# Handing the first stage's rows to the second stage inside SBUF, and one table tile behind the first weights

## The chip, the cores and the metric

The kernel runs on one core of one Trainium2 chip. The metric is the device time of one execution in microseconds. Five engines work side by side, each through its own instructions in order: TensorE (PE, matrix products), VectorE (DVE), ScalarE (ACT), GpSimd (POOL) and SyncE (SP). SP, ScalarE and GpSimd also issue transfers (DMA) between DRAM and SBUF, the memory on the core; products land in PSUM, a small memory of banks, and must be copied out ("evicted") from there.

## What is computed

```python
x = randn(8, 3008, 256) * 0.1          # batch, sequence, dimension
X = np.fft.fft(np.fft.fft(x, axis=1), axis=2).real        # FNet mixing
h = X.reshape(24064, 256) @ w_in                          # w_in 256 x 2048
g = h * np.clip(h + 3.0, 0.0, 6.0) / 6.0                  # hard swish
out = g @ w_out                                           # w_out 2048 x 256
```

So the kernel takes the real part of a two-dimensional Fourier transform of each of 8 sequences and sends all 24064 rows through a two-layer network. [...]

## The kernel before

**The stages.** The sequence length is 47 * 64. Stage 1 is a transform of length 47 over rows that are first folded (sums and differences of mirrored columns, on VectorE for the first sequence, on GpSimd later); its result z holds, in its partitions, the 48 rows (24 frequencies, real and imaginary) of two blocks, and for each of them some columns n2. Stage 2 is a transform of length 64 over n2, so it needs the n2 in the partitions: the rows change places. That is done by transfers: z goes to a DRAM tile zd and comes back as a tile g. Stage 2 multiplies g by a table T (one slice per group `gr` of frequencies; a slice for both sides of the frequency, with zeros in the quadrants that don't belong) and leaves q; the row qn is the last row of q, spread over all partitions. The transform along the 256 columns is folded into w_in (`fold_w_in`, by the table C), giving W1 and its last row WN, which `send_wn` sends from a row to a column by small transfers on SP.

**The network.** The rows are worked on in chunks (`Chunk`) of four frequencies, each in eight steps `fc` over the 2048 hidden columns. A step is `mlp1` (products u and v of W1 with q on TensorE, then `activate`: s, sum, difference and gates on VectorE, the relu on ScalarE, leaving a), `combine` (sums c of parts of a, on GpSimd) and `mlp2` (products of G, the turned w_out, with a and c). In the first chunk `mlp2_first` does without c.

**The weights.** The 16 pieces of w_in and w_out (`PIECES`: two of w_in, two of w_out, and so on) are loaded by `load_w(j)` and turned by five helpers, one for each engine's part: `exponent_a` (ScalarE, two passes of 128x512), `exponent_b` (two products on TensorE), `exponent_c` (a copy on ScalarE), `mantissa` (two passes on VectorE) and `join` (VectorE, gives wi or a block of G). `fold_w_in(j)` makes W1 of a piece of w_in.

**The order.** Nothing is scheduled automatically: `manual_schedule` keeps the order in which the program text issues instructions, engine by engine. The start-up is written out by hand: eight gathers of x (each 128 rows of 1024 floats) from GpSimd, folds on VectorE, four rounds of stage 1 (`FIRST`) with `evict_first` one round behind, then the exchange through DRAM, stage 2 of groups 0 and 1, and the first chunk's steps with the weight pieces between them (`first_steps`, `second_steps`). `beside(p)` lists what else is issued at which step: `put(t, f, ...)` at step t. `LATER` names the steps at which rows of later groups go from z to zd.

**What the change touches.** `evict_first` copies a round of stage 1 from PSUM to z (112 partitions) and sends the rows of groups 0 and 1 to zd at once, those of later groups when `LATER` says so. `load_g_half` reads a group of zd back into g. `both_tables` gives the slice of T for both sides. `load_t` loads a slice of T, for groups 0 and 1 from ScalarE's and GpSimd's queue in the start-up. `clear_table` writes the zero quadrants, for slices 0 and 1 on ScalarE. `keep_awake` are products of zeros that keep TensorE running. `spare` are two PSUM banks used by turns.

Of the kernel before, what the change touches and what calls it, by code (L numbers as in the profile page):

```python
# [7 lines left out]
F32 = mybir.dt.float32  # L8
# [50 lines left out]
def kernel(  # L59
# [30 lines left out]
    NG = NCK // 2  # L90
    NSG = 4
    NIX = NP * NXC
    DH = 32
# [162 lines left out]

    later, middle = {}, []

# [86 lines left out]
    def evict_first(hb, m, ps, pt):  # L345
        k = FIRST.index(m)
        pool, tag = ((zpool, "z"), (zpool, "z"), (apool, "a"), (cpool, "c"))[k]
        z = pool.tile([PX, 2, 2, D + 1], F32, tag=tag, name="z")
        for h in range(2):
            nc.scalar.copy(z[:, h, :, D:], pt[h][0:PX])  # L350
        nc.scalar.copy(z[:, 0, :, 0:D], ps[0][0:PX])
        (nc.vector.tensor_copy if k == NM - 1 else nc.scalar.copy)(z[:, 1, :, 0:D], ps[1][0:PX])
        if not first.zd:
            first.zd[0] = dpool.tile([NG, 2 * KK, 2, NS, D + 1], F32, tag="zd0", name="zd")
        zd = first.zd[0][:].rearrange("g k c (h n) d -> (g k c) h (n d)", h=2)
        n0 = 2 * 4 * KK
        for i in range(2):
            n = (m * XC + 2 * i) * (D + 1)
            for j in range(PZ // n0):
                dst = zd[j * n0:(j + 1) * n0, :, n:n + 2 * (D + 1)]  # L360
                rs = slice(i * PB + j, i * PB + 2 * n0, 2) if j < 2 else slice(i * PB + 2 * n0, i * PB + PZ)
                src = z[rs].rearrange("p h n d -> p h (n d)")
                if j == 0:
                    (nc.scalar if k == NM - 1 and i else nc.sync).dma_start(out=dst, in_=src)
                else:
                    later.setdefault((j, k), []).append((dst, src))

# [68 lines left out]

    def both_tables(gr, blk, u):
# [4 lines left out]
    def stage2_half(hb, gr, copy=nc.scalar.copy, ps=None):  # L442

        vg, i = hb.b * NSG // 2 + gr // 2, gr % 2
        if i == 0:
            first.q[vg] = qpool.tile([P, 2, 2 * TB], F32, tag="q", name="q")
        g = hb.g[gr]
        if starting[0] and ps is None:
            for u in range(KK):
                ps = bank([P, 2, P], "ps2")  # L450
                for blk in range(2):
                    nc.tensor.matmul(ps[:, blk].rearrange("p (b k) -> p b k", b=2),
                                     g[:, u, blk * (P + 1):blk * (P + 1) + P], both_tables(gr, blk, u),
                                     start=True, stop=True)
                copy(first.q[vg][:, :, u * P:(u + 1) * P], ps[:])
            return
        ps = bank([P, 2, TB], "ps2") if ps is None else ps
        for u in range(KK):
            for blk in range(2):
                nc.tensor.matmul(ps[:, blk, u * P:(u + 1) * P].rearrange("p (b k) -> p b k", b=2),  # L460
                                 g[:, u, blk * (P + 1):blk * (P + 1) + P], both_tables(gr, blk, u),
                                 start=True, stop=True)
        copy(first.q[vg][:, :, i * TB:(i + 1) * TB], ps)
# [13 lines left out]

    def spread_by_pe(hb, ps, copy=nc.scalar.copy):
        row_tile(first, 0)
        for u in range(KK):  # L480
            nc.tensor.matmul(ps[:, u * P:(u + 1) * P], hb.g[0][:, u, D:D + 1].to_broadcast([P, P]),
                             both_tables(0, 1, u), start=True, stop=True)
        copy(first.qn[0][:, 0:TB], ps)
        del hb.g[0]
# [273 lines left out]
    def exponent_b(j):  # L758
        pm = [PM[j % len(PM)][:, i].bitcast(F16) for i in range(2)]
        if j == 3:  # L760
            exs[j] = spare[1][:].rearrange("p i n -> p (i n)")
        elif starting[0] or j == 4:
            exs[j] = ps_h.tile([P, WB], F32, tag="uv", name="ex")[:]
        elif j % 2 == 0:
            exs[j] = bank([P, WB], "ex")[:]
        else:

            exs[j] = spare[1 if j % 4 == 1 else 0][:].rearrange("p i n -> p (i n)")
        for i in range(2):
            nc.tensor.matmul(exs[j], E[:, i], pm[i], start=(i == 0), stop=(i == 1))  # L770
# [42 lines left out]
    def fold_w_in(j):  # L813
# [7 lines left out]
        for blk in range(2):  # L821
            for i in range(2):
                nc.tensor.matmul(ps[:, blk], C[:, i, blk * P:(blk + 1) * P], wi[:, i], start=(i == 0), stop=(i == 1))  # L823
        (nc.vector.tensor_copy if j == 0 else nc.scalar.copy)(W1[:, :, fc * nb:(fc + 1) * nb], ps[:])
        for f in range(2 * fc, 2 * fc + 2):
# [85 lines left out]
    nc.gpsimd.dma_start(out=C[:], in_=c_dim)  # L911
# [12 lines left out]
    exponent_c(0)  # L924
    clear_table(1, slice(0, 2))
    for k, m in enumerate(FIRST):
# [5 lines left out]
    for k, m in enumerate(FIRST):  # L932
# [22 lines left out]
    join(1)  # L955
    see(w[PIECES[1]][:, 0:1])
    load_w(3)
    for j in range(4, 10):
# [12 lines left out]
    starting[0] = False  # L971
# [6 lines left out]
    def beside(p):  # L978
# [7 lines left out]
        if p == 0:  # L986
            for gr in range(2, NG):
                put(gr, load_t, gr)
            put(2, spread_half, halves[0], 1)
# [71 lines left out]

    def first_steps(s):
        j = 2 * s + 4
        more = j < len(PIECES)
        if s == 0:

            mlp2_first(*chunk(s), halves=(0,))
        else:
            mlp2_first(*chunk(s - 1), halves=(1,))
        if more:
            exponent_b(j)
            exponent_b(j + 1)
            exponent_c(j)
            if s > 0:
                join(j)
                tail(j + 1)  # L1080
                exponent_a(j + 2)
        if s > 0:
            mlp1(*chunk(s + 1))
        else:
            activate(*chunk(s + 1), *uv, between=lambda: join(j))
            tail(j + 1)
            exponent_a(j + 2)
        mlp2_first(*chunk(s), halves=(1,) if s == 0 else (0, 1))
        if s == 0:
            fold_w_in(j)  # L1090
        if more:
            exponent_b(j + 2)
            exponent_c(j + 2)
            exponent_a(j + 3)
            if s > 0:
                fold_w_in(j)
            fold_w_in(j + 1)
            if s > 0:
                exponent_b(j + 3)

# [30 lines left out]

    LATER = {1: ((1, 2), (2, 2)), 3: ((1, 0), (1, 1), (1, 3)), 5: ((2, 0), (2, 1), (2, 3))}

# [32 lines left out]
def _tables(B, S, D):  # L1166
# [18 lines left out]
    f0 = np.zeros((2, 64, 8, 64))  # L1185
    f0[:, :N1, :, :2 * NK1] = g[:, :, np.r_[np.arange(32).reshape(2, 16).T.ravel(), 32:2 * NK1]].swapaxes(0, 1)
    f[2:5:2] = f[2:5:2, ::-1]
# [5 lines left out]
    for i in range(B):  # L1193
# [22 lines left out]
    co, si = cs(np.outer(np.arange(D), np.arange(D)), D)  # L1216
    d = np.concatenate([co[:, :h], -si[:, 1:h], co[:, h:h + 1]], axis=1) / WS
    return {
        "c_stage1": f.astype(np.float32),
        "c_stage2": t.reshape(N2, 2, NK1 // 4, 4, N2).transpose(2, 0, 1, 3, 4).astype(np.float32),  # L1220
        "c_dim": d.reshape(2, h, D).swapaxes(0, 1).astype(np.float32),
    }
# [31 lines left out]
```

## Time and profile before

| | |
|---|---|
| median of 3 runs | 1931.37 us (1930.52 to 2507.39) |
| profiled execution, its own time | 1931.23 us |
| its span, first to last instruction | 1929.5 us |
| TensorE busy | 1914.8 us, 99% of the span |
| VectorE, GpSimd, ScalarE busy | 1429.4, 1448.3, 679.5 us |
| granted TensorE clock, mean | 0.999 |
| bytes moved | 98.22 MB, mean 51 GB/s |
| transfers in the first of 40 slices (48 us) | 270 GB/s |

The durations below come from the one profiled execution. A row of the timeline has the start in microseconds from the span's start, the time to the end of the group, the engine (with a q: its issuing of transfers), the line, the operation, what it writes and reads, and in brackets how long the engine had been idle and what ended that. Groups of small products overlap a little, so the start of the next group is the better measure of how long one takes. A row of waits has the total, the number and the longest.

### The profile page before, as it was taken

What the parts mean: (1) busy time and instruction counts of PE and PEld (TensorE: products, weight loads), DVE (VectorE), ACT (ScalarE), POOL (GpSimd) and SP (SyncE); (2) the same over time, 40 slices, a digit from 0 to 9 for tenths busy, and PEclk for the clock granted to TensorE, in tenths of its full rate; (3) what the DMA queues carried; (4) which work ended last, traced back from release to release, by engine and by line L of the source; (5) the groups of instructions that cost most, each with busy time, mean ns of one, the idle gap of its engine ahead of it and who ended that gap; (6) DMA issues with size and microseconds to landing.
All of it is one profiled execution on the core that took longest, in us unless ns stands there. A gap on an engine that the chain in (4) does not pass through costs nothing.

```text
span 1929.5 us, 28305 instructions
## 1 busy us (share of the span) xinstructions
PE 1914.8 (99%) x9398; PEld 1650.7 (86%) x9398; DVE 1429.4 (74%) x2754; ACT 679.5 (35%) x1167; POOL 1448.3 (75%) x1656
## 2 busy tenths in 40 slices
PE   8999999999999999999999999999999999999998
PEld 5688888888988888888898888888899888888888
DVE  7867776777777777777787777777778777777777
ACT  6533333333333333333333333333333333333332
POOL 5697888896688778787678877878666667666765
PEclk9999999999999999999999999999999999999999
DMA  8432232211112222121111221221110101101000
GB/s 270 122 88 51 61 82 65 64 44 40 30 37 71 56 52 56 45 55 36 28 37 50 51 56 44 53 53 50 36 28 20 28 17 27 35 12 28 18 21 20
DMA packets 154985, 98.22 MB, mean 51 GB/s; under 512 B 122335, under 2 KB 136394, under 8 KB 154838
## 3 DMA queue, kind: packets, MB, share of 16 engines
q1 hardware_dynamic: 142166, 57.55, 12.4%
q0 software_dynamic: 11216, 37.94, 6.7%
q8 instruction: 74, 1.21, 0.3%
q10 hardware_dynamic: 1456, 0.92, 0.2%
q14 instruction: 73, 0.60, 0.1%
HBM read 59.87 MB, written 37.32 MB: 50 GB/s over the span
## 4 chain that ended last, share of the span: by engine, by line
PE 95%; DVE 3%; ACT 1%; issue 0%; DMA 0%; POOL 0%; DVEq 0%; ACTq 0%; POOLq 0%
PE acc L646 56%; PE v L551 17%; PE u L551 16%; PE ps L499 2%; PE acc L626 1%; PE ps L276 1%; DVE a L602 1%; PE spare L823 1%; DVE s L560 0%; ACT t L599 0%; DMA xt<-in_x_dram,IT 0%; DVE o L707 0%; DVE u L583 0%; PE ps L460 0%; PE ps L377 0%
## 5 line engine op out<-in xcount | busy, mean ns | idle before, releaser
L616 POOL TENSOR_TENSOR c<-a 128x512 f32<-128x512 f32 (+1 forms) x375 | 469.3, 1251 | 358.7 <-PE acc L646 307.1
L646 PE MATMUL acc<-c,G 128*128 128x256 f32 (+1 forms) x3008 | 697.2, 375 | 0.0
L599 ACT ACTIVATE t<-u,half 128x512 f32<-128x512 f32 (+1 forms) x384 | 260.7, 679 | 1142.3 <-DVE u L570 1063.0
L646 PEld LDWEIGHTS acc<-c,G 128*128 128x128 f32 x3008 | 565.2, 190 | 71.5 <-POOL c L616 0.4
L560 DVE SCALAR_TENSOR_TENSOR s<-qn,WN,u 128x256 f32<-128x256 f32 (+1 forms) x768 | 330.2, 471 | 340.9 <-PE u L551 340.4
L646 PE MATMUL acc<-a,G 128*128 128x256 f32 (+1 forms) x2256 | 541.6, 376 | 0.0
L646 PEld LDWEIGHTS acc<-a,G 128*128 128x128 f32 x2256 | 421.0, 189 | 73.6 <-issue 20.1
L551 PE MATMUL v<-q,W 127*128 127x256 f32 (+1 forms) x1536 | 389.2, 375 | 1.5 <-DVE a L602 1.5
L551 PE MATMUL u<-q,W 128*128 128x256 f32 (+1 forms) x1536 | 388.0, 375 | 0.0
L602 DVE SCALAR_TENSOR_TENSOR a<-t,u 128x512 f32<-128x512 f32 (+2 forms) x448 | 263.8, 601 | 101.1 <-ACT t L599 97.3
L551 PEld LDWEIGHTS v<-q,W 127*128 127x128 f32 x1536 | 288.0, 190 | 41.8 <-DVE a L602 1.9
L551 PEld LDWEIGHTS u<-q,W 128*128 128x128 f32 x1536 | 285.9, 190 | 37.3 <-issue 2.6
L616 POOL TENSOR_TENSOR c<-c,a 128x256 f32<-128x256 f32 (+1 forms) x375 | 269.1, 717 | 29.4
L616 POOL TENSOR_TENSOR c<-a,c 128x256 f32<-128x256 f32 (+1 forms) x375 | 268.9, 717 | 29.4
L570 DVE TENSOR_TENSOR u<-s,v 128x512 f32<-128x512 f32 x352 | 245.1, 696 | 37.0 <-DVE s L560 0.5
L602 DVE SCALAR_TENSOR_TENSOR a<-t,v 128x512 f32<-128x512 f32 (+1 forms) x480 | 263.3, 565 | 0.1
L599 ACT ACTIVATE t<-v,half 128x512 f32<-128x512 f32 (+1 forms) x384 | 260.7, 679 | 0.2 <-issue 0.2
L572 DVE TENSOR_TENSOR v<-v,s 128x512 f32<-128x512 f32 x352 | 243.8, 693 | 0.0
L616 POOL TENSOR_TENSOR r<-w,e 128x256 f32<-128x256 f32 (+1 forms) x92 | 88.9, 987 | 3.6
L656 ACT ACTIVATE e<-acc 128x512 f32<-128x512 f32 (+2 forms) x184 | 83.5, 545 | 0.0
L707 DVE STREAM_TRANSPOSE o<-r 128x256 f32<-128x256 f32 (+1 forms) x192 | 72.5, 415 | 0.3
L616 POOL TENSOR_TENSOR w<-w,e 128x512 f32<-128x512 f32 (+1 forms) x46 | 57.5, 1251 | 3.6
(128 smaller groups left out, 779.0 us busy)
## 6 DMA issues: line engine op xcount, KB each, us to landing
out_dram<-o SPq DMA_DIRECT2D x744, 32.0 KB
g<-zd SPq DMA_DIRECT2D x42, 256.0 KB
zd<-z SPq DMA_DIRECT2D x48, 192.0 KB
xt<-in_x_dram POOLq DMA_DIRECT2D x21, 256.0 KB, 3.8
st<-in_moe_w_out_dram POOLq DMA_DIRECT2D x8, 512.0 KB, 7.0
qn<-qd SPq DMA_DIRECT2D x16, 256.0 KB
st<-in_moe_w_in_dram POOLq DMA_DIRECT2D x7, 512.0 KB, 6.9
xt<-in_x_dram POOLq DMA_DIRECT2D x17, 192.0 KB, 4.1
```

Source lines behind the costliest of these rows:

```text
L276: nc.tensor.matmul(ps[b][h * PB:(h + 1) * PB, 0:n], F[rows(b), 0:PB], y[rows(b), 2 * h:2 * h + n], start=True, stop=not last, skip_group_c ...
L499: nc.tensor.matmul(ps[:, blk, u * P:n].rearrange("p (b k) -> p b k", b=2), g[:, kk, blk * (P + 1):blk * (P + 1) + P], T[:, :, gr, blk, kk, ...
L551: nc.tensor.matmul(ps[:, i, 0:nq], W1[r, blk, f * P:(f + 1) * P], q[r, blk, of:of + nq], start=True, stop=True)
L560: nc.vector.scalar_tensor_tensor(s[:, i, 0:nq], qn[:, of:of + nq], WN[:, f:f + 1], u[:, i, 0:nq], op0=AL.mult, op1=AL.add)
L570: nc.vector.tensor_tensor(u[:], s[:], v[:], op=AL.add)
L572: nc.vector.tensor_tensor(v[:], v[:], s[:], op=AL.subtract)
L599: nc.scalar.activation(t, h, AF.Relu, bias=half[:], scale=scale)
L602: nc.vector.scalar_tensor_tensor(dst, t, 1.0, h, op0=AL.min, op1=AL.mult)
L616: (eng or nc.gpsimd).tensor_tensor(out, in0, in1, op=AL.add)
L646: nc.tensor.matmul(ch.acc[i // 2][:, i % 2, 0:ch.n], G[:, i, fc, :], mv, start=(fc == 0 and i % 2 == 0), stop=(fc == NF - 1), skip_group_c ...
L656: nc.scalar.mul(ch.e[:, k:i + 1, 0:ch.n], ch.acc[i // 2][:, 0:i + 1 - k, 0:ch.n], 1.0 / WS)
L707: nc.vector.transpose(o[:, 0:n // DH, h], ch.r[:, m, h, 0:n].rearrange("p (j i) -> p j i", i=DH))
```

## The change

Rows of groups 0 and 1 no longer go through DRAM. Each round's z now has all 128 partitions, and for each of the two groups and each of its two pairs of frequencies one transfer (`turn_first`) takes 8 partitions of z (1028 floats each) and writes 32 partitions of g (257 floats each). The order of frequencies within the stage 1 table is changed on the host so that this is one regular pattern. The transfers are on SP, one of them on ScalarE. The rows of the other four groups go to zd as before, in twice as many transfers of half the rows, and `LATER` spreads them over steps 1 to 6.

Slices 0 and 1 of T are no longer loaded or cleared in the start-up. A tile TF with the table of those two groups, zeros included (128 x 1024 floats, from the host), is loaded on GpSimd's queue between the second piece of w_in and the first piece of w_out. Slices 0 and 1 of T, which the second sequence needs, are cleared on GpSimd at step 9 and loaded at steps 14 and 15; the clearing of the other slices is divided over steps 1 and 2.

The order behind stage 1 is written anew: stage 2 of group 0 comes ahead of the second fold of w_in and ahead of the third piece's exponents, and the conversions of pieces 2 to 5 move with it. Only the copy of the second fold is cut in two, with an exponent copy between the halves.

```diff
@@ evict_first
-        z = pool.tile([PX, 2, 2, D + 1], F32, tag=tag, name="z")
+        z = pool.tile([P, 2, 2, D + 1], F32, tag=tag, name="z")
...
-        zd = first.zd[0][:].rearrange("g k c (h n) d -> (g k c) h (n d)", h=2)
-        n0 = 2 * 4 * KK
-        for i in range(2):
-            n = (m * XC + 2 * i) * (D + 1)
-            for j in range(PZ // n0):
-                dst = zd[j * n0:(j + 1) * n0, :, n:n + 2 * (D + 1)]
-                rs = slice(i * PB + j, i * PB + 2 * n0, 2) if j < 2 else slice(i * PB + 2 * n0, i * PB + PZ)
-                src = z[rs].rearrange("p h n d -> p h (n d)")
-                if j == 0:
-                    (nc.scalar if k == NM - 1 and i else nc.sync).dma_start(out=dst, in_=src)
-                else:
-                    later.setdefault((j, k), []).append((dst, src))
+        for gr in range(2):
+            for u in range(KK):
+                turns[gr, k, u] = hb.g[gr][m:P:NM, u, :], z[gr * KK + u:P:NQ].rearrange("p h n d -> p (h n d)")
+        zd = first.zd[0][:].rearrange("g k c (h n) d -> g (k c) h (n d)", h=2)
+        for gr in range(2, NG):
+            n0 = 2 * 2 * KK
+            for i in range(2):
+                n, r = (m * XC + 2 * i) * (D + 1), i * PB + (gr - 2) * NQ + 2 * KK
+                later.setdefault((gr // 2, k), []).append((zd[gr, :, :, n:n + 2 * (D + 1)],
+                                                           z[r:r + n0].rearrange("p h n d -> p (h n d)")))
+
+    def turn_first(gr, k, last=nc.sync):
+        for u in range(KK):
+            to, fr = turns.pop((gr, k, u))
+            (last if u else nc.sync).dma_start(out=to, in_=fr)
@@ fold_w_in
+        if j == 1:
+            for blk in range(2):
+                nc.scalar.copy(W1[:, blk, fc * nb:(fc + 1) * nb], ps[:, blk])
+                if blk == 0:
+                    exponent_c(2)
@@ start-up
     load_w(1)
+    TF = apool.tile([P, 2, 2, KK, 2 * N2], F32, tag="a", name="TF")
+    nc.gpsimd.dma_start(out=TF[:].rearrange("p g b u k -> p (g b u k)"), in_=c_dim[:, 2 * D:])
     load_w(2)
-    load_t(1, queue=nc.gpsimd)
...
-    load_t(0, queue=nc.scalar)
     mantissa(0)
     exponent_b(0)
-    keep_awake(2)
-    clear_table(0, slice(0, 2))
+    keep_awake(1)
+    keep_awake(1, TB)
     exponent_c(0)
-    clear_table(1, slice(0, 2))
...
             evict_first(hb, FIRST[k - 1], *before)
+            for gr in range(2 if k < NM - 1 else 1):
+                turn_first(gr, k - 1)
...
     evict_first(hb, m, *before)
-    load_g_half(hb, 0)
-    load_g_half(hb, 1)
+    turn_first(0, k, nc.scalar)
+    turn_first(1, k - 1)
     mantissa(1)
     fold_w_in(0)
+    turn_first(1, k)
     exponent_a(1)
+    keep_awake(1)
     exponent_b(1)
     exponent_c(1)
-    exponent_a(2)
-    keep_awake(1)
     join(1)
...
     mantissa(2)
-    fold_w_in(1)
-    exponent_b(2)
-    stage2_half(hb, 0)
-    exponent_c(2)
-    spread_by_pe(hb, bank([P, TB], "ps3")[:])
-    join(2)
-    exponent_a(3)
-    mantissa(3)
+    stage2_half(hb, 0, tab=TF)
+    spread_by_pe(hb, bank([P, TB], "ps3")[:], TF)
+    exponent_a(2)
@@ beside
+            for gr in range(2):
+                put(14 + gr, load_t, gr)
...
-                put(1, clear_table, b, slice(2, NG), nc.gpsimd)
+                put(1, clear_table, b, slice(2, 4), nc.gpsimd)
+                put(2, clear_table, b, slice(4, NG), nc.gpsimd)
+                put(9, clear_table, b, slice(0, 2), nc.gpsimd)
@@ ahead of the steps
     uv = mlp1_products(*chunk(0))
+    exponent_b(2)
     activate(*chunk(0), *uv)
     ps = spare[0]
-    stage2_half(halves[0], 1, copy=lambda o, i: None, ps=ps)
+    stage2_half(halves[0], 1, copy=lambda o, i: None, ps=ps, tab=TF)
+    nc.scalar.copy(first.q[0][:, :, TB:], ps[:])
+    mantissa(3)
+    fold_w_in(1)
+    join(2)
+    exponent_a(3)
     head(4)
-    nc.scalar.copy(first.q[0][:, :, TB:], ps[:])
-    exponent_b(3)
-    head_b(5)
     uv = mlp1_products(*chunk(1))
-    tail(3)
-    exponent_a(5)
@@ first_steps, s == 0
             mlp2_first(*chunk(s), halves=(0,))
+            exponent_b(3)
+            exponent_b(j)
+            exponent_c(j)
+            exponent_c(3)
+            exponent_a(j + 1)
+            activate(*chunk(s + 1), *uv, between=lambda: join(j))
+            mlp2_first(*chunk(s), halves=(1,))
+            exponent_b(j + 1)
+            head_b(j + 1)
+            tail(j + 1)
+            join(3)
+            exponent_a(j + 2)
+            fold_w_in(j)
+            exponent_b(j + 2)
+            exponent_c(j + 2)
+            exponent_a(j + 3)
+            fold_w_in(j + 1)
+            return
@@ LATER
-    LATER = {1: ((1, 2), (2, 2)), 3: ((1, 0), (1, 1), (1, 3)), 5: ((2, 0), (2, 1), (2, 3))}
+    LATER = {1: ((1, 2), (2, 2)), 2: ((1, 0),), 3: ((1, 1), (1, 3)), 4: ((2, 0),), 5: ((2, 1),), 6: ((2, 3),)}
```

More of the change, by code (lines that the diff above doesn't have):

```diff
@@ L91 @@
     NSG = 4
+    NQ = PB // 4
     NIX = NP * NXC
@@ L255, in fold @@
         del pr.x[c], pr.xr[c]
-    later, middle = {}, []
+    later, middle, turns = {}, [], {}
     starting = [True]
@@ L435, in load_g_half, with both_tables @@
         hb.g[gr] = g
-    def both_tables(gr, blk, u):
+    def both_tables(gr, blk, u, tab=None):
+        if tab is not None:
+            return tab[:, gr, blk, u]
         t = T[:, :, gr, blk, 2 * u]
@@ L440, in both_tables, with stage2_half @@
         return bass.AP(t.tensor, t.offset, [p, [b[0] + step, b[1]], k])
-    def stage2_half(hb, gr, copy=nc.scalar.copy, ps=None):
+    def stage2_half(hb, gr, copy=nc.scalar.copy, ps=None, tab=None):
         vg, i = hb.b * NSG // 2 + gr // 2, gr % 2
@@ L949 @@
     fold_w_in(0)
+    turn_first(1, k)
     exponent_a(1)
+    keep_awake(1)
     exponent_b(1)
     exponent_c(1)
-    exponent_a(2)
-    keep_awake(1)
     join(1)
     see(w[PIECES[1]][:, 0:1])
-    load_w(3)
-    for j in range(4, 10):
+    for j in range(3, 10):
         load_w(j)
@@ L1077, in first_steps @@
             exponent_c(j)
[L1078 to L1085, printed above, removed]
+            join(j)
             tail(j + 1)
             exponent_a(j + 2)
-        mlp2_first(*chunk(s), halves=(1,) if s == 0 else (0, 1))
-        if s == 0:
-            fold_w_in(j)
+        mlp1(*chunk(s + 1))
+        mlp2_first(*chunk(s))
         if more:
@@ L1217, in _tables @@
     d = np.concatenate([co[:, :h], -si[:, 1:h], co[:, h:h + 1]], axis=1) / WS
+    t = t.reshape(N2, 2, NK1 // 4, 4, N2).transpose(2, 0, 1, 3, 4)
+    tf = np.zeros((2, 2, 2, 2, 2, 4, 2, 2, 2, 2, N2))
+    for b in range(2):
+        rows = t[0:2, :, :, b::2].reshape(2, 2, 2, 4, 2, 2, 2, 2, N2)
+        tf[:, b, :, :, :, :, :, :, :, b] = rows.transpose(4, 1, 2, 5, 3, 0, 6, 7, 8)
+    d = np.concatenate([d.reshape(2, h, D).swapaxes(0, 1).reshape(h, -1), tf.reshape(h, -1)], axis=1)
     return {
         "c_stage1": f.astype(np.float32),
-        "c_stage2": t.reshape(N2, 2, NK1 // 4, 4, N2).transpose(2, 0, 1, 3, 4).astype(np.float32),
-        "c_dim": d.reshape(2, h, D).swapaxes(0, 1).astype(np.float32),
+        "c_stage2": t.astype(np.float32),
+        "c_dim": d.astype(np.float32),
     }
```

39 lines of the change are left out of this document (20 added, 19 removed).

## The prediction, made before the changed kernel ran

> **What bounds the kernel now.** I read first the page, then TensorE's waits over the whole span, then the stretches of the start-up, and at last the start-up in order of time.
>
> ```profile
> span 1929.5 us, 28305 instructions
> PE 1914.8 (99%) x9398; PEld 1650.7 (86%) x9398; DVE 1429.4 (74%) x2754; ACT 679.5 (35%) x1167; POOL 1448.3 (75%) x1656
> PE 95%; DVE 3%; ACT 1%; issue 0%; DMA 0%; POOL 0%; DVEq 0%; ACTq 0%; POOLq 0%
> ...
> PE v L551 <- DVE a L602: 1.5, 5, 0.7
> PE acc L626 <- DVE a L602: 1.2, 1, 1.2
> ```
>
> TensorE is 99% busy and 95% of the chain that ended last. Its named waits are a few single microseconds, and nearly all of them lie in the first 70 us, before the two-layer product runs evenly. The change touches nothing behind that point but side work, so it can only move the moment from which TensorE is never idle again; what it wins or loses there comes out once, at the end, one for one. 2% of the run is 38.6 us, about what a measurement of this kernel can tell from no change; the whole start-up holds less than that in waits.
>
> The start-up has two parts. The first is paced by the gathers of x, which VectorE folds as they land:
>
> ```profile
> 11.76 0.69 DVE L203 TENSOR_TENSOR xt<-xt 111x508 f32<-111x508 f32 x1 [1.43 <-DMA xt<-in_x_dram,IT]
> ...
> 13.36 0.69 DVE L203 TENSOR_TENSOR xt<-xt 111x508 f32<-111x508 f32 x1 [0.19 <-DMA xt<-in_x_dram,IT]
> ```
>
> From 13.36 us on the folds follow each other to the end of stage 1 and TensorE follows them. The second part runs from the last eviction (20.9 us) to the first expert product:
>
> ```profile
> 20.91 0.69 DVE L352 COPY z<-ps 112x512 f32<-112x512 f32 x1
> 21.68 0.67 ACTq L364 DMA_DIRECT2D zd<-z  x1
> 22.45 1.40 ACT L756 ACTIVATE PM<-st,bias 128x512 uint8<-128x512 int16 x2 [0.99 <-DVE top L781]
> 23.90 0.38 PE L770 MATMUL ex<-PM,FI 128*128 128x512 f16 x1 [0.27 <-ACT PM L756]
> 24.65 0.91 SPq L432 DMA_DIRECT2D g<-zd  x2
> 25.76 1.96 PE L823 MATMUL wps<-wi,C 128*128 128x256 f32 x8 [0.63 <-DVE wi L790]
> 27.56 0.59 PE L770 MATMUL ex<-PM,FI 128*128 128x512 f16 x2
> 27.99 1.05 PE L452 MATMUL ps<-T,g 128*128 128x128 f32 x8
> 28.88 0.61 PE L481 MATMUL ps<-T,g 128*128 128x128 f32 x4
> 29.51 1.13 PE L551 MATMUL u<-q,W 128*128 128x256 f32 x4
> 30.48 1.03 PE L551 MATMUL v<-q,W 127*128 127x256 f32 x4
> 31.34 1.06 PE L460 MATMUL spare<-T,g 128*128 128x128 f32 x8
> 32.23 0.59 PE L770 MATMUL spare<-PM,FI 128*128 128x512 f16 x2
> 32.67 1.03 PE L551 MATMUL u<-q,W 128*128 128x256 f32 x4
> ```
>
> The evicted rows go to DRAM (L364) and come back (L432); the way back is issued at 24.65 us. While it runs, TensorE does the second weight fold (25.76) and an exponent pair (27.56), so it meets stage 2 (27.99) without a named wait. The round trip is hidden, but only behind work that stands ahead of stage 2.
>
> **The change part by part.** *First, the table slices ahead of the weights.* ScalarE's queue (q10) loaded slice 0 of T while the gathers (q0) were still coming in:
>
> ```profile
> q0 software_dynamic: 317, 0.83, 74.6%
> q10 hardware_dynamic: 158, 0.26, 27.7%
> ```
>
> These are the transfer queues between 7.5 and 11.5 us: together they fill the 16 transfer engines, and the table took 27.7% of 4 us, 1.1 us. Without it the third and fourth gathers land up to 1.1 us sooner. VectorE's waits on them (1.43 + 0.19 = 1.62 us) allow all of it, since it is free from 11.76 - 1.43 = 10.3 us on. Bounds: 0 (the gap has another cause) to -1.1. Against it stand the new transfers: 32 rows of 1028 bytes where there were 32 of 2056, twice as many, through the same 16 engines during the last gathers. I take -0.9. The bytes of both slices come back as TF, on GpSimd's queue behind the first weights and ahead of w_out's first piece. The last transfer of that queue so far was slice 1:
>
> ```profile
> L830 POOL DMA_DIRECT2D T<-in_c_stage_dram x2: 628/630/632, 14.6 to 15.1; - x2
> ...
> DMA to landing us min/median/max: 8.6/8.7/8.8
> ```
>
> It landed by 23.7 us, and now the weight piece is the last, after the same bytes, TF before it. They are needed from about 24.6 and 25.5 on, so I price the order at nothing (cover: 1 to 2 us; a later landing is paid in full).
>
> *Second, z straight into g.* One transfer takes the place of two. The old first leg is the nearest row: issued by 21.68 + 0.67 = 22.35, landed when SP goes on at 24.65, hence 2.3 us. Bounds: 1.9, where the exponents take over (next sentence but one), and 6.2 (a rival). The last pair of the first group is issued at the same place (one by SP, one by ScalarE), so g[0] is there at 24.65 on the old clock. The exponent pair ahead of it ends at 23.90 + 0.38 = 24.28. Stage 2 starts at 24.65 instead of 27.99, 3.3 us sooner.
>
> [...]
>
> *Third, the new order.* The second fold (25.76 to 27.56, 1.8 us) and the exponent pair (0.43 us) now come behind the first u and v; nothing is saved on TensorE, only the gap ahead of stage 2. From 24.65: stage 2 0.89, spread 0.45, a wait of 0.3 for the copies, u 0.86, v 0.86, exponents 0.43, group 1 0.89, the fold 1.72, its first half's copy 0.3: the second u near 31.4 instead of 32.67, 1.3 us sooner. The old order then lost 1.22 us to VectorE, which was still with the first chunk:
>
> ```profile
> 31.87 0.86 DVE L560 SCALAR_TENSOR_TENSOR s<-qn,WN,u 128x256 f32<-128x256 f32 x2
> 35.78 1.96 PE L626 MATMUL acc<-a,G 128*128 128x512 f32 x4 [1.22 <-DVE a L602]
> 38.34 0.87 DVE L560 SCALAR_TENSOR_TENSOR s<-qn,WN,u 128x256 f32<-128x256 f32 x2
> 42.31 0.68 DVE L790 TENSOR_TENSOR wi<-top,spare 128x512 f32<-128x512 f32 x1
> 43.51 1.89 PE L823 MATMUL spare<-wi,C 128*128 128x256 f32 x8
> 45.24 1.88 PE L626 MATMUL acc<-a,G 128*128 128x512 f32 x4
> ```
>
> That stall goes, since the first chunk's s now starts near 27.3, with its u. But what is late next is the second chunk. Its s needs two rows of WN, which SP can only send when the fold's two half copies are done (32.0, an exponent copy stands between them). A WN transfer takes about 2.4 us to land:
>
> ```profile
> 43.89 3.40 SPq L811 DMA_DIRECT2D WN<-W  x4
> ...
> 49.24 0.19 POOL L897 COPY seen<-WN 128x1 f32<-128x1 f32 x1 [6.01 <-DMA WN<-W]
> ```
>
> (of these four issues the third, which GpSimd waits for, ends near 46.7; GpSimd goes on at 49.24). So the second s starts at 35.0 instead of 38.34. From s to the end of the fifth piece's wi it was 42.31 + 0.68 - 38.34 = 4.65 us; now one mantissa more (1.07) stands inside, and its relu waits on ScalarE behind two exponent copies and a 1.4 us exponent step (1.2). 35.0 + 4.65 + 1.07 + 1.2 = 41.9 instead of 42.99: 1.1 us. Here the orders join again: the fold at 43.51 and m2 at 45.24 come 1.1 us sooner, and from there on TensorE has the old sequence. Bounds of this part: -2.7 (ScalarE does not stand in the way, the gain at 35.78 is kept) to +2.8, below.
>
> *What costs nothing.* Group 1's last pair is behind two WN issues on SP, near 24.5, and lands by 27, while its product comes at about 28.8. Eviction of 128 rows instead of 112 takes the same columns. TensorE's filler products move inside its waits. The later zd rows are 32 issues instead of 16 on SP at 2.52 / 4 = 0.63 us each, 10 us more, spread over steps 1 to 6, and the WN of the next folds stand behind the first eight; SP idles there, and g of group 2 is read far later. GpSimd's zero fill grows by ScalarE's share and two of its parts move:
>
> ```profile
> 48.39 2.52 SPq L1146 DMA_DIRECT2D zd<-z  x4
> ...
> 39.58 3.65 POOL L878 MEMSET T<- 64x2048 f32 x2
> 106.36 0.72 POOL L616 TENSOR_TENSOR c<-a,c 128x256 f32<-128x256 f32 x1
> ...
> 110.66 1.03 PE L646 MATMUL acc<-c,G 128*128 128x256 f32 x4
> ```
>
> Half of 3.65, 1.8 us, now sits in front of the c that ends at 107.08 and is read from 110.66: 3.6 us of room; if that were gone it would cost up to 1.8. Slices 0 and 1 of T are loaded at steps 14 and 15, for step 26.
>
> **The sum.** -0.9 (gathers) - 1.1 (from eviction to the fifth piece) = -2.0 us. The profiled execution took 1931.23 us, 1.7 outside its span of 1929.5, and lies 0.1 under the median of 1931.37. So 1931.2 - 2.0 = 1929.2 us.
>
> **The rivals.** *The gathers don't land sooner* (the change does not do what it says): the moved bytes delay them as TF, or the new rows do. Only the second part is left, 1930.1. For it: as many bytes come back; against it: they come behind the gathers, and the two queues' shares add up to 102%.
>
> *ScalarE does not stand in the way*: the whole lead at 35.78 is kept, -0.9 - 2.7, 1927.6. For it: ScalarE is only 35% busy over the span. Against it, its share in the stretches concerned (8.39 of 10 us):
>
> ```profile
> 40.00:50.00 10.00, 9.55 (x37) 6.21 (x36) 8.71 (x19) 8.39 (x14) 3.56 (x4) 1.00 0.42 143
> ```
>
> *The direct transfer is slow*, on the other side. A small transfer on SP's queue has taken far longer:
>
> ```profile
> SPq L475 <- DMA qd<-q: 5.7, 1, 5.7
> ```
>
> That is one wait, under a full load of weight transfers. With 5.7 + 0.5 = 6.2 us instead of 2.3, stage 2 starts at 28.55, later than it did, with the moved 2.2 us of work still to come: 41.9 + 3.9 - 42.99 = +2.8, less 0.9: 1933.1, slower. It decides from a landing of 4.3 us on (2.3 + 0.9 + 1.1). For it: TF and a weight piece are in flight then. Against it: the old leg, in the same place and under nearly the same load, took 2.3.
>
> **How the numbers follow.** My forecast 0.5, no sooner gathers 0.15, ScalarE out of the way 0.2, slow transfer 0.15. The low end takes the gains together (-1.1 - 2.7 - 0.4 for the earliest landing: 1927.0) and half the 0.85 us between the lowest run and the median, 1926.6; the high end, 1932.6, stops short of the slow transfer's 1933.1, of whose landings the shorter ones lie inside. The forecast's own range is 1928.0 to 1930.3. None of the cases comes near 38.6 us, so within 2% gets 0.97; 0.01 is left for faster, 0.02 for slower (an unseen wait that returns at every step).
>
> **What would show it.** Right: VectorE's waits on the gathers fall by about 1 us, stage 2 begins near 23.7, the second u near 30.5, the m2 of 45.24 near 43.2, no new TensorE wait behind 70 us. Wrong: a TensorE wait on a transfer ahead of stage 2, on TF, or on WN; a second s that is not near 34; a c that TensorE waits for at step 10.

## The result: 9 us slower, and the profile after

| | before | changed |
|---|---|---|
| median | 1932.15 us | 1941.26 us |
| lowest | 1930.52 us | 1938.39 us |
| ratio, 95% interval | | 1.0041 [1.0029, 1.0054] |
| profiled execution, its span | 1929.5 us | 1938.1 us |

The forecast was 1929.2 us, 1926.6 to 1932.6. The change costs 0.4%: within 2%, but on the other side of no change and outside the range. One run of the kernel before, of 2507.39 us, is not in the ratio; so the medians are 9.1 us apart where the ratio says 7.9.

The page of the changed kernel first: the engines' busy time and the chain of what ended last.

```profile
PE 1917.7 (99%) x9398; PEld 1652.8 (85%) x9398; DVE 1432.8 (74%) x2754; ACT 677.4 (35%) x1166; POOL 1449.7 (75%) x1659
PE 95%; DVE 2%; DMA 1%; ACT 1%; issue 0%; ACTq 0%; SPq 0%; DVEq 0%
```

The chain now has 1% of transfers (0% before), and TensorE is busy 2.9 us longer for the same products. The next view is TensorE's waits (total, times, longest):

```profile
PE spare L827 <- DVE wi L794: 4.0, 1, 4.0
PE v L557 <- DVE a L608: 3.6, 5, 2.8
```

Two single waits are new or longer: one of 4.0 us ahead of the fold of piece 4, and one of 2.8 us for v (0.7 before). Pieces are counted from 0, as in the code; the fold at 43.51 that the prediction calls the fifth piece's is that of piece 5. The start-up in order of time (names as in the prediction; line numbers are 1 to 6 higher):

```profile
19.73 0.69 DVE L353 COPY z<-ps 128x512 f32<-128x512 f32 x1
21.72 1.18 ACTq L370 DMA_DIRECT2D g<-z  x1
23.00 1.40 ACT L762 ACTIVATE PM<-st,bias 128x512 uint8<-128x512 int16 x2 [2.72 <-DVE W L834]
24.66 1.13 PE L458 MATMUL ps<-TF,g 128*128 128x128 f32 x8
31.76 1.13 PE L557 MATMUL u<-q,W 128*128 128x256 f32 x4 [0.46 <-ACT W L830]
32.52 1.18 SPq L815 DMA_DIRECT2D WN<-W  x2
38.94 0.48 DVE L566 SCALAR_TENSOR_TENSOR s<-qn,WN,u 128x256 f32<-128x256 f32 x1 [4.74 <-DMA WN<-W]
40.20 0.48 DVE L566 SCALAR_TENSOR_TENSOR s<-qn,WN,u 128x256 f32<-128x256 f32 x1 [0.79 <-DMA WN<-W]
43.13 3.78 PE L827 MATMUL spare<-wi,C 128*128 128x256 f32 x8 [3.96 <-DVE wi L794]
50.10 1.88 PE L632 MATMUL acc<-a,G 128*128 128x512 f32 x4
75.88 1.50 PE L557 MATMUL v<-q,W 127*128 127x256 f32 x4 [2.79 <-DVE a L608]
77.17 4.96 PE L632 MATMUL acc<-a,G 128*128 128x512 f32 x8
81.97 0.59 PE L774 MATMUL ex<-PM,FI 128*128 128x512 f16 x2
```

Up to the second u all is sooner than before: the last eviction by 1.2 us, stage 2 by 3.3, the second u by 0.9. Then the second chunk's s waits for the two WN rows that SP issued from 32.52 on. Its two halves start at 38.94 and 40.20, as the rows land; the wi of piece 4 is late behind s, and TensorE stands still for 3.96 us. In the windows the granted clock is the third number from the end of a row (ahead of the transfer share and GB/s):

```profile
30.00:40.00 10.00, 8.34 (x29) 4.32 (x27) 4.61 (x9) 7.18 (x13) 4.46 (x6) 1.00 1.01 374
40.00:50.00 10.00, 6.87 (x18) 5.14 (x19) 8.98 (x17) 5.58 (x9) 2.81 (x3) 0.66 0.43 146
...
70.00:80.00 10.00, 7.21 (x20) 3.79 (x19) 9.47 (x17) 4.35 (x8) 8.47 (x13) 0.83 0.43 81
```

The clock falls to 0.66 and 0.83 in the two stretches with the two waits, and so the fold takes 3.78 us instead of 1.9 and the m2 of 77.17 takes 4.96 instead of 3.60. The loss adds up point by point, against the rows of the prediction and of the same view before the change: the m2 (mlp2's products) of 45.24 starts at 50.10 (+4.86); v of 68.96 at 75.88 (+2.07 more, the wait 2.79 instead of 0.72); the next exponents at 81.97 instead of 73.36 (+1.69 more, the clock). Together 8.6 us, the whole difference of the two spans.

### The profile page after: what moved, and what is told of

Its sections match the earlier page's. It is cut to its first block, busy times and chain, and to the rows that moved or that the text cites. A ratio compares the mean times of both kernels' runs of the same rounds, so it can differ in the third digit from the quotient of the medians.

```text
span 1938.1 us, 28339 instructions
## 1 busy us (share of the span) xinstructions
PE 1917.7 (99%) x9398; PEld 1652.8 (85%) x9398; DVE 1432.8 (74%) x2754; ACT 677.4 (35%) x1166; POOL 1449.7 (75%) x1659
## 4 chain that ended last, share of the span: by engine, by line
PE 95%; DVE 2%; DMA 1%; ACT 1%; issue 0%; ACTq 0%; SPq 0%; DVEq 0%
PE acc L652 56%; PE v L557 16%; PE u L557 16%; PE ps L505 2%; PE ps L277 1%; PE acc L632 1%; DVE a L608 1%; PE spare L827 1%; DVE s L566 0%; ACT t L605 0%; DMA WN<-W 0%; DVE o L713 0%; DMA g<-z 0%; DVE u L589 0%; PE ps L466 0%
```

## What was tried

Each kernel starts from the changed one. The last column is the median less that of the kernel before, measured together with it; the changed kernel itself has +9.1. An interval reaches some 2 us to either side, so gains of 1 to 2 us below are read from the traces; the times alone don't show them.

| kernel | median | ratio to before, 95% interval | us |
|---|---|---|---|
| zero fill at step 1 | 1936.49 | 1.0023 [1.0014, 1.0033] | +5.2 |
| weights held back | 1936.51 | 1.0024 [1.0014, 1.0033] | +5.2 |
| WN 2, 3 by TensorE | 1935.79 | 1.0018 [1.0009, 1.0028] | +4.5 |
| fillers | 1938.91 | 1.0036 [1.0023, 1.0049] | +7.6 |
| both repairs | 1933.93 | 1.0008 [0.9999, 1.0018] | +2.0 |
| fold first | 1935.25 | 1.0013 [1.0003, 1.0023] | +3.3 |
| SP unloaded | 1934.10 | 1.0020 [1.0006, 1.0033] | +2.2 |
| slice ahead again | 1941.94 | 1.0053 [1.0035, 1.0070] | +10.0 |
| repairs, relu first | 1932.14 | 1.0001 [0.9992, 1.0010] | +0.5 |
| repairs, fill at 23 us | 1931.84 | 0.9998 [0.9989, 1.0007] | +0.2 |
| repairs, both of these | 1931.89 | 0.9997 [0.9988, 1.0006] | +0.3 |
| the same, pair by GpSimd | 1930.92 | 0.9993 [0.9984, 1.0002] | -0.7 |

**Is it the load on the transfer engines?** Weight pieces 6 to 9 are held back until WN row 3 has landed:

```diff
-    for j in range(3, 10):
+    for j in range(3, 6):
         load_w(j)
...
     fold_w_in(1)
+    see(WN[:, 3:4])
+    for j in range(6, 10):
+        load_w(j)
```

> The changed kernel with the weight pieces 6 to 9 sent by GpSimd only when WN row 3 has landed (they follow pieces 3 to 5 at once in the changed kernel). Theory A (the two WN transfers of the second fold, 128 packets of 4 bytes each, stand in transfer engines filled by the weight pieces): they land within about 2.5 us of their issue at 32.5 and 33.1, the second chunk's s starts near 35.5 instead of 38.9 and 40.2, TensorE's 3.96 us wait ahead of the fold at 43.13 falls under 1 us and the granted clock stays 1.00; m2 of 50.10 near 44.5, some 5 us less, 1936 us (pieces 8 and 9 landing late would give part of it back). Rival B (a WN transfer takes 6 us whatever else moves): s stays near 39 to 40 and the time at 1941 or, since the weights are later too, above.

```profile
34.34 1.18 SPq L815 DMA_DIRECT2D WN<-W  x2
37.27 0.87 DVE L566 SCALAR_TENSOR_TENSOR s<-qn,WN,u 128x256 f32<-128x256 f32 x2 [1.41 <-DMA WN<-W]
```

From the first issue to both rows it is 2.9 us here and 7.7 us in the changed kernel (32.52 to 40.20). Same transfer, same queue, same place in the program; only weight pieces 6 to 9 are missing (the transfer engines are 65% busy from 30 to 40 us, 101% in the changed kernel). So the weight pieces queued behind are the cause, and 6 us whatever moves is refuted. The gain is 3.9 us in the difference to before, with 5 expected: in this profiled execution the clock was 0.83 between 20 and 30 us, the second u came at 33.58 instead of 31.76, and m2 at 46.21, not near 44.5. The wait of v is still there.

**Is it WN at all?** The two columns are made where they are needed:

```diff
+        if j == 1:
+            col = spare[0]
+            for f in range(2):
+                for i in range(2):
+                    nc.tensor.matmul(col[:, 0, f:f + 1], wi[:, i, f * P:(f + 1) * P], C[:, i, D - 1:D],
+                                     start=(i == 0), stop=(i == 1))
+            return
...
     join(2)
+    nc.vector.tensor_copy(WN[:, 2:4], spare[0][:, 0, 0:2])
```

> The changed kernel with columns 2 and 3 of WN not transferred: four TensorE products of one column each make them behind the second fold, and VectorE copies them from PSUM ahead of s. Theory A (the wait on WN is the loss): second s near 34.8 us instead of 38.9 and 40.2, no wait over 1 us ahead of the fold at 43.13, clock 1.00 between 40 and 50, m2 of 50.10 near 44; about 6 us less, 1935 us, with the later wait of v (2.79 us) still there in part. Rival B (ScalarE's order or the clock, not WN, holds the fold): s early, but the fold still after 42 us, 1940 us or more.

```profile
36.15 0.87 DVE L566 SCALAR_TENSOR_TENSOR s<-qn,WN,u 128x256 f32<-128x256 f32 x2
46.66 1.88 PE L632 MATMUL acc<-a,G 128*128 128x512 f32 x4
```

No wait on WN, no wait over 0.4 us ahead of the folds, clock 1.00 from 30 to 50 us. m2 comes at 46.66 instead of 44. This execution's second half of group 1's rows landed late (1.32 us of waiting at 31.00) and the columns cost TensorE 0.95 us, so the second u comes at 34.06; behind it VectorE waits 1.68 us for ScalarE's relu, of which more below. The wait on WN, with the clock lost behind it, is worth 4.6 us, some three quarters of what was expected of it.

**What does the clock cost?** Eight products without use fill TensorE's wait:

```diff
+            for i in range(8):
+                nc.tensor.matmul(spare[0][:, 0], ones[:], W1[:, 0, 0:TB], start=True, stop=True)
             fold_w_in(j)
```

> The changed kernel with eight products without use (0.43 us each, 3.4 us) in TensorE's wait ahead of the fold at 43.13. Theory A (the wait itself lowers the granted clock, to 0.66 between 40 and 50 us, and the slow products behind it are a cost of their own): clock 1.00, the fold 1.9 instead of 3.78 us, m2 of 50.10 at 47.9, where VectorE's wi then sets it: 2.2 us less, 1939.1 us. Rival B (VectorE sets the fold and m2 anyway, the clock costs nothing): m2 stays at 50.1, 1941.3 us.

```profile
43.38 2.00 PE L827 MATMUL spare<-wi,C 128*128 128x256 f32 x8 [0.75 <-DVE wi L794]
48.26 1.88 PE L632 MATMUL acc<-a,G 128*128 128x512 f32 x4
74.15 1.13 PE L557 MATMUL v<-q,W 127*128 127x256 f32 x4 [2.78 <-DVE a L608]
```

The fold starts as late as in the changed kernel (43.38), takes 2.00 us instead of 3.78 at a clock of 1.00 between 40 and 50 us, and m2 starts 1.84 us sooner; the forecast was 47.9 and 1939.1. So in these two profiles some 3.0 us of the first loss are the wait and 1.8 us the clock that the wait leaves behind. The time agrees (1.5 us less in the difference to before), but the intervals overlap, and this profile is the fastest of six executions.

**Where does the second wait come from?** The changed kernel fills groups 4 and up of T with zeros at step 2. VectorE's two mantissa operations are slow in the stretch that follows; the groups of the lines view (times, then busy us and mean ns) over the eight instructions ahead of that chunk's s, before the change and after it:

```profile
L782 DVE SCALAR_TENSOR_TENSOR top<-st,top 128x512 f32<-128x512 uint32 x4 | 3.3, 828 | 0.1
L781 DVE TENSOR_SCALAR top<-st 128x512 int32<-128x512 int32 x4 | 2.6, 652 | 0.0
```

```profile
L786 DVE SCALAR_TENSOR_TENSOR top<-st,top 128x512 f32<-128x512 uint32 x4 | 4.5, 1135 | 0.1
L785 DVE TENSOR_SCALAR top<-st 128x512 int32<-128x512 int32 x4 | 3.4, 852 | 0.0
```

7.9 us instead of 5.9, and the wait of v grew by 2.07. The fill itself is over by then, but GpSimd's adds behind it begin 6.8 us later than before the change (61.84, 55.03), where TensorE is only 4.9 late:

```profile
59.92 1.95 POOL L888 MEMSET T<- 64x1024 f32 x2
61.84 0.72 POOL L809 TENSOR_TENSOR G<-G 128x256 f32<-128x256 f32 x1
```

The experiment puts the fill back to step 1:

```diff
-                put(1, clear_table, b, slice(2, 4), nc.gpsimd)
-                put(2, clear_table, b, slice(4, NG), nc.gpsimd)
+                put(1, clear_table, b, slice(2, NG), nc.gpsimd)
```

> The changed kernel with GpSimd's zero fill of table groups 4 and up back at step 1 (as before the change; groups 0 and 1 stay at step 9). Theory A (the second lost stretch, v waiting 2.79 us at 75.88, comes from the zero fill that was moved to step 2: it pushes GpSimd's adds under VectorE's eight mantissa steps, which then take 7.9 us instead of 5.9): that wait falls to about 0.7 us, the granted clock stays 1.00 between 70 and 80 us, the products behind it take 3.6 instead of 4.96 us; 3.7 us less, 1937.6 us. Rival B (that stretch is an echo of the late WN rows alone): wait and clock stay, 1941.3 us. In both the wait of second s on WN stays at 38.9 and 40.2 us.

```profile
L786 DVE SCALAR_TENSOR_TENSOR top<-st,top 128x512 f32<-128x512 uint32 x4 | 3.3, 828 | 0.1
L785 DVE TENSOR_SCALAR top<-st 128x512 int32<-128x512 int32 x4 | 2.6, 648 | 0.0
```

The eight instructions are back at 5.9 us, v waits 1.09 us, the clock is 1.00 between 70 and 80, and m2 behind it takes 3.60 us. The time is 3.9 us less, with 3.7 expected. So the place of the fill is shown to be the cause of the second wait. Beside GpSimd's adds (of G and xt, in the changed kernel) both mantissa operations are slow, up to 1.05 and 1.23 us instead of 0.42 and 0.69; beside a fill (in the kernel with both repairs, below) the first takes 2.05 us and the second its usual 0.69. Why the two kinds of work differ no run shows.

**Both repairs together.** The column by TensorE and the fill at step 1.

> Both repairs together: the zero fill back at step 1 and columns 2 and 3 of WN made by TensorE. Theory A (the two losses are separate: the late WN rows, which alone gave 5.5 us, and GpSimd under VectorE's mantissas, which alone gave 4.8): no wait on WN, v's wait of 2.79 us under 1.2, clock 1.00 from 30 to 90 us; 1941.3 - 5.5 - 4.8 = 1931 us, level with the kernel before. Rival B (one loss seen twice): the gains don't add, 1935 us.

+2.0 us: neither 1931 nor 1935. Against the kernel before, measured together with them, the two gave 3.9 and 4.6 of 9.1 us (the 4.8 and 5.5 of the expectation compare medians taken at two times, between which the kernel before had moved by 0.8), so 0.6 would be left. The gains nearly add, so they are two losses. Whether a rest stays the time doesn't say: the interval holds 0.6 us and, just, no change. The trace has rows that a rest could come from:

```profile
24.43 1.40 ACT L762 ACTIVATE PM<-st,bias 128x512 uint8<-128x512 int16 x2 [2.94 <-DVE W L834]
...
41.15 0.69 DVE L608 SCALAR_TENSOR_TENSOR a<-t,u 128x512 f32<-128x512 f32 x1 [1.67 <-ACT t L605]
44.84 3.83 POOL L895 MEMSET T<- 64x2048 f32 x2
44.88 2.05 DVE L785 TENSOR_SCALAR top<-st 128x512 int32<-128x512 int32 x1
46.96 0.69 DVE L786 SCALAR_TENSOR_TENSOR top<-st,top 128x512 f32<-128x512 uint32 x1
54.48 1.13 PE L557 MATMUL v<-q,W 127*128 127x256 f32 x4 [0.81 <-DVE a L608]
```

Three things: VectorE waits 1.67 us for ScalarE's relu; the fill holds a mantissa step of 0.42 us for 2.05; and ScalarE's exponents of piece 1 start 2.8 us after the last eviction has ended.

**Two that didn't answer.** *SP unloaded*: as both repairs, the first two columns of WN by TensorE too, and the last transfers of group 1 sent ahead of the first fold.

```diff
-        if j == 1:
-            col = spare[0]
+        if j < 2:
+            col = spare[0] if j else ps
...
+    turn_first(1, k)
     mantissa(1)
     fold_w_in(0)
-    turn_first(1, k)
```

> As the kernel with both repairs, but the first two columns of WN are made by TensorE too and the last two transfers of z into the second group's g are sent before the first fold, not behind WN rows 0 and 1: SP issues them at 24.2 instead of 25.4 to 26.2 us. Theory A (those two transfers also fall into the weight pieces: in three of the five profiles so far the second group's stage 2 waits on them, up to 1.5 us): no wait of TensorE on a transfer at 28 to 32 us, second u near 31.8 each time, about 1 us less than with both repairs alone, 1930 us. Rival B (that wait is chance and costs nothing in the median): level with both repairs alone.

No wait on those transfers, but +2.2 against +2.0: the forecast gain is not there, and in the profile of both repairs that wait was absent too. So the wait comes in some executions only, and no cost of it shows in the median. Two of this kernel's ten executions took 1941.17 and 1943.97 us; no profile shows why. *Fold first*: the fill at step 1, and the second fold, its copy in one piece again, moved ahead.

```diff
...
     spread_by_pe(hb, bank([P, TB], "ps3")[:], TF)
+    fold_w_in(1)
     exponent_a(2)
...
-    fold_w_in(1)
+    exponent_c(2)
```

> The zero fill back at step 1 and the second weight fold back ahead of the first chunk's u (behind stage 2 and the spread), so that SP sends WN rows 2 and 3 some 4 us sooner, before the weight pieces fill the transfer engines; the rest of the change stays. Theory A (the move of the fold behind u and v is the step that made WN late): first u about 28 us, second s near 35 to 36 instead of 38.9 and 40.2, no clock loss between 40 and 50; 1931 to 1932 us. Rival B (the direct transfers or the missing table slice are what costs): as with the zero fill alone, 1936.5 us.

+3.3, between the two. WN rows were issued at 34.24 and s waited for the second until 42.28, 8.0 us: the earlier place still lies under the weight pieces (transfer engines 67% busy from 30 to 40 us, 82% from 40 to 50). This profiled execution had a clock of 0.57 from 20 to 30 us, so its times are no measure of the rest. Inconclusive on the order.

**The table slice.** Slice 0 is loaded on ScalarE's queue again, ahead of the folds, and no longer at step 14.

```diff
     exponent_a(0)
+    load_t(0, queue=nc.scalar)
     mantissa(0)
...
```

> The changed kernel with slice 0 of the table loaded on ScalarE's queue ahead of the gathers' folds again, as before the change (it isn't read there: TF stays, and the load at step 14 is left out). Theory A (that slice delays the gathers): VectorE waits on the gathers again, the last copy of stage 1 starts about 1 us later than the 19.5 to 20.1 us seen so far, the time is 0.5 to 1.2 us above the changed kernel's 1941.3. Rival B (the gathers' gap has another cause): no difference in either.

```profile
9.68 0.69 DVE L204 TENSOR_TENSOR xt<-xt 111x508 f32<-111x508 f32 x1 [0.34 <-DMA xt<-in_x_dram,IT]
21.87 0.69 DVE L353 COPY z<-ps 128x512 f32<-128x512 f32 x1 [0.79 <-PE ps L342]
```

The folds have a gap again and the last eviction starts at 21.87; in the eleven profiles of the changed kernel and of those without that load it started between 19.51 and 21.10 us (fold first, with its half clock, left out). That is for theory A, but it doesn't show it: gaps occur without that load too (0.72 us with the relus first), the kernel before, which has the load, started at 20.91, inside that range, and the 0.9 us more in time lie inside the intervals. Whether the slice delays the gathers stays open.

**The rest of 2 us.** The relus ahead of the exponents of piece 5, with both repairs:

```diff
-            exponent_a(j + 1)
             activate(*chunk(s + 1), *uv, between=lambda: join(j))
+            exponent_a(j + 1)
```

> Both repairs (zero fill at step 1, WN columns 2 and 3 by TensorE), and ScalarE's exponent step of piece 5 behind the second chunk's two relus instead of ahead of them. Theory A (what is left, 1933.9 against 1931.9 us, is ScalarE's order: VectorE waits 1.67 us for the relu at 41.15, the sixth piece's wi comes at 43.61 instead of 42.31 before the change): that wait under 0.5 us, m2 of 46.18 near 44.8, 1.0 to 1.4 us less, 1932.7 us. Rival B (the exponents of piece 5 then come 1.4 us later and hold the same fold): no difference, 1933.9 us.

VectorE's wait for the relu is 0.39 us, m2 starts at 45.25 instead of 46.18, and 1.5 us of the 2.0 are gone in time. The zero fill near 23 us instead:

```diff
     mantissa(1)
+    see(fracs[1][:, 0:1])
+    for b in range(2):
+        clear_table(b, slice(0, NG), nc.gpsimd)
     fold_w_in(0)
...
```

> Both repairs, and GpSimd's whole zero fill of the table (all groups) when VectorE has done piece 1's mantissa, near 23 us, where GpSimd and nearly VectorE are idle, instead of steps 1 and 9. Theory A (the fill slows VectorE wherever they meet: one mantissa step of 0.42 us took 2.05 us at 44.88 beside it, and v then waits 0.81 us at 54.48): that step back at about 0.5 us, no wait of v at 54, 0.8 us less than with both repairs, 1933.1 us. Rival B (VectorE has slack there): no difference; or, if the fill delays the weight pieces behind it, up to 1 us more.

The mantissa step at 45.11 takes 0.42 us, v at 54 doesn't wait, and 1.8 us are gone in time, over twice the forecast. Both together:

> Both repairs with both of these: the relus first and the zero fill near 23 us. Theory A (two separate rests): 1933.9 - 1.2 - 0.8 = 1931.9 us, level with the kernel before. Rival B (one rest, or none): 1933 us or more.

+0.3 us: the time came out as expected, but it is no better than either alone, so theory A's two separate rests are not shown. Perhaps each frees the same stretch of VectorE; but the early fill also has a price in this profile, where it holds the mantissa step of piece 2 at 25.90 for 2.08 us, and TensorE then waits 0.68 us at 32.21. No run separates the two. Last, the pair that ScalarE sent:

```diff
-    turn_first(0, k, nc.scalar)
+    turn_first(0, k, nc.gpsimd)
```

> As the kernel with both orders, and the last transfer of z into the first group's g is sent by GpSimd instead of ScalarE. Theory A (ScalarE's send stands in front of the exponents of piece 1: it starts 1.3 to 1.5 us after the eviction has ended and takes 1.18 us, before the change 0.67 us with no such wait, and so stage 2 starts 5.0 us behind the last eviction's start instead of the 3.7 us of my sum): exponents of piece 1 over 1.5 us sooner after the eviction, stage 2 about 4.2 us behind it, 0.7 us less, 1931.2 us. Rival B (GpSimd's transfer lands later than ScalarE's): TensorE waits on the transfer ahead of stage 2, 1 us or more above the kernel with both orders.

```profile
19.53 0.69 DVE L353 COPY z<-ps 128x512 f32<-128x512 f32 x1
19.97 1.45 ACT L762 ACTIVATE PM<-st,bias 128x512 uint8<-128x512 int16 x2
24.27 1.13 PE L458 MATMUL ps<-TF,g 128*128 128x128 f32 x8 [1.38 <-DMA g<-z]
```

The exponents start at once, 3.0 us sooner than in the changed kernel, and the median is 1.0 us lower than with both orders. Stage 2 now waits for the transfer, 4.7 us behind the eviction's start and not 4.2. It is 0.7 us under the kernel before, but its interval includes 1: it can't be told from no change.

## Why the prediction was wrong

**The step that failed: a WN transfer takes 2.4 us.** The prediction took this from four issues at 43.9 us, when the weight pieces had landed (transfer engines 7% busy from 44 to 46 us), for a transfer that was to start at 32 us, in the middle of them. In the changed kernel the two transfers took 6.4 and 7.1 us from issue to s. So the second chunk's s, forecast near 34, started at 38.94 and 40.20, and the m2 of 45.24, forecast near 43.2, at 50.10. The trace of before had the right price. Issues of the kernel before, then the two queues in the windows 32 to 34 and 34 to 36 us (packets, MB, share of the 16 engines):

```profile
25.60 3.94 SPq L811 DMA_DIRECT2D WN<-W  x4
...
q0 software_dynamic: 211, 0.74, 102.5%
q1 hardware_dynamic: 139, 0.00, 4.2%
...
q0 software_dynamic: 202, 0.76, 95.9%
q1 hardware_dynamic: 149, 0.00, 4.4%
```

The last two of these four are issued from 28.37 to 29.54, and their packets move from 32.3 to 35.9 us: over 5 us from the first of these issues to the last packet there too. It cost nothing, since s needed them at 38.34. In the changed kernel, issued from 32.52 to 33.70, none moves from 34 to 36; they move in the windows 36 to 38 and 38 to 40:

```profile
q0 software_dynamic: 217, 0.77, 101.5%
...
q0 software_dynamic: 204, 0.76, 100.0%
q1 hardware_dynamic: 146, 0.00, 4.6%
...
q0 software_dynamic: 215, 0.76, 98.7%
q1 hardware_dynamic: 142, 0.00, 4.5%
```

The prediction even quoted a small transfer of 5.7 us under that load and used it as a rival for the rows of g. It was the right mechanism at the wrong place: 5.7 us in place of 2.4 for WN makes s 3.3 us later and turns the sum from -2.0 into +1.3 us, above the time of before. The rest of the miss is in the next two steps.

**The clock was no term of the sum.** A stall was priced at its length. In the profiles 3.96 us of it cost 1.8 more, and the second one 1.7 more. The seven executions of the changed kernel differ the same way: from 1938.39 us at a mean clock of 0.998 to 1942.39 at 0.995.

**"GpSimd's zero fill costs nothing" looked at one place.** The c that TensorE reads at step 10 does not wait, as said. But the part at step 2 pushes the adds under VectorE's mantissas, 2.1 us. The prediction named GpSimd's own reader and not the engine beside it; and the change does touch TensorE behind 70 us, through this side work.

**Stage 2 at 23.7: it came at 24.66.** Stage 1 ended 1.2 us sooner in this execution, with VectorE folding without a wait (-0.9 had been priced; by the table slice's experiment the reason stays open). But stage 2 starts 4.9 us behind the eviction's start instead of 3.7: ScalarE's send begins 1.3 us after the eviction has ended and takes 1.18 us instead of 0.67, and the exponents stand behind it. Why the send begins so late no run shows. The 2.3 us were a landing, without the wait to issue, and as a landing they hold: where stage 2 did wait for a transfer of z that ScalarE sent (WN by TensorE, both orders), it went on 2.1 and 2.2 us after the send's end.

**What was right.** The stall of 1.22 us went, m2 of 35.78 starts at 33.59; the second u came sooner (31.76; 30.5 said); no wait on TF, none at step 10; ScalarE did stand in the way of the second chunk's relu, 1.67 us (1.2 said), once WN was out of it. "No new TensorE wait behind 70 us" was wrong. Of the signs that were to show the forecast wrong two appeared: an s far from 34, and a wait on WN, though it is VectorE that waits for it and TensorE for VectorE.

**Where the gain went.** With both losses repaired and the orders mended the kernel is level with the one before: 3 us or so won ahead of stage 2 buy nothing that the times can tell. With the relus first, the row of v is

```profile
69.19 1.13 PE L557 MATMUL v<-q,W 127*128 127x256 f32 x4 [0.95 <-DVE a L608]
```

so TensorE still arrives there ahead of VectorE, as it did before at 68.96 (0.72 us). What TensorE wins ahead of that point it waits for here. That this pace is set by VectorE's and ScalarE's conversions of the weights, from 64-bit floats to 32-bit ones, is argued from these rows, not shown by a run. In the last kernel v comes at 67.78 (0.69 us of waiting), 1.2 us sooner than before the change, so there some of the lead gets through.

## What to carry to other kernels

Price a transfer at the load of the moment it moves to, not where it was last seen (here 6.4 and 7.1 us in place of 2.4): look up in the windows which queue fills the engines then, and read when the packets of a like transfer moved, even if nobody waited for them. When work moves out of the way of one engine, ask what else is still queued on the others at that time, and which engine runs beside the moved part. A stall of TensorE can be dearer than its length: here one of 3.96 us cost 1.8 us more and one of 2.79 us 1.7 more, with the clock at 0.66 and 0.83 in the 10 us around them. Eight products without use in the first of these stalls kept the clock of its 10 us at 1.00, which shows what the clock costs while the cause is sought.

## What was not expected of the hardware

Two rows of 512 bytes on SP's queue took 2.9 us from the first issue to use with the later weight pieces held back, and 7.7 us with them. The 7.7 us have two parts. The first packet moves at 36.4, 3.9 us after the first issue. Between 37 and 39 us the packets of WN and of the weights move in nearly equal numbers, 204 and 203; the first of these two microseconds:

```profile
q0 software_dynamic: 100, 0.37, 100.9%
q1 hardware_dynamic: 99, 0.00, 6.5%
```

So the two rows, 288 packets, take 3.3 us, to 39.7. At 99 in a microsecond they would take 2.9 us (an estimate from this row). The wait of 3.9 us ahead of the first packet is not explained by these numbers; where the packets stood no run here shows.

The clock behind the wait of 3.96 us, in a window of 2 us:

```profile
44.00:46.00 2.00, 2.00 (x6) 1.53 (x6) 1.86 (x4) 1.02 (x2) 0.11 (x1) 0.50 0.00 0
```

The granted clock is 0.50 there. The wait of v, 2.8 us, was followed by 0.83 between 70 and 80 us in three profiles (the changed kernel, weights held back, WN by TensorE) and by 1.00 in two (fillers, slice ahead). So a wait of the same length goes with a lower clock in some executions and not in others, and no run here shows what decides.
